# First tile's PSUM copy moved to ScalarE, norm offsets moved to GpSimd, and dummy matmuls behind the first transposes

## The chip, the cores and the metric

The kernel runs on one core of one Trainium2 chip. The metric is the device time of one execution in microseconds (us); lower is better. The profile's span is about 1.8 us shorter than the device time of the same execution. A run is called slow when it is over 1.5% above the fastest run of the same kernel.

A kernel is a list of instructions for five engines: TensorE (PE; its weight loads are PEld), VectorE (DVE), ScalarE (ACT), GpSimd (POOL) and SyncE (SP, which issues the DMAs). The order in which each engine's instructions are issued is not written by hand here. The program is written once from top to bottom, and a list scheduler in the compiler's front end sorts the instructions of each engine by its own cost estimates.

## The reference

The reference is a layernorm, a non-causal linear attention with 32 heads, a residual, a second layernorm and a gated feed-forward part (S = 2048 tokens, D = 1024, F = 3584). Only the beginning matters here.

```python
def _layernorm(x, axis=-1, eps=1e-5):
    m = jnp.mean(x, axis=axis, keepdims=True)
    v = jnp.var(x, axis=axis, keepdims=True)
    return (x - m) / jnp.sqrt(v + eps)

x = A_x
h = x + _A_ref(_layernorm(x, axis=-1), A_wqkv, A_wo)   # qkv = x @ wqkv, phi(k)^T v, ...
h2 = h + _B_ref(_layernorm(h, axis=-1), B_W_gate, B_W_up, B_W_down)
return h2
```

## The kernel before

Sixteen token tiles of 128 rows are normalized and transposed, so that they can be the stationary operand of the k and v products. The first four tiles are transposed by TensorE through PSUM, half by half, the others by DMA. The first four tiles use plain products (`kp`, `vp`). Later ones use Strassen's scheme: seven products of half size, whose operands are sums made on VectorE (`left_sums`, and `sums` in `right_ops`) and whose results are combined from PSUM by ScalarE copies (`m`, `u`, line 154) and VectorE sums (line 211).

```python
# per tile t (lines 266-291)
for k in range(2):
    nc.vector.bn_stats(out=stats[:, k, :], in_=x_sb[:, k * NW:(k + 1) * NW])          # L272
nc.vector.bn_aggr(out=mv[:], in_=stats[:])                                            # L274
nc.scalar.activation(out=lnv, in_=mv[:, 1:2], func=ACT.Ln, bias=LN_EPS, scale=1.0)    # L277
nc.scalar.activation(out=rstd, in_=lnv, func=ACT.Exp, scale=-0.5)                     # L278
if t == atiles[0]:
    ...                                  # tile 0: normalized by VectorE, no offset needed (L283)
nc.vector.scalar_tensor_tensor(out=nmr, in0=mv[:, 0:1], scalar=-1.0, in1=rstd,        # L287, offset
                               op0=ALU.mult, op1=ALU.mult)
nc.scalar.activation(out=xn[:], in_=x_sb[:], func=ACT.Identity, bias=nmr, scale=rstd) # L288
if t not in atiles[:PE_T]:
    nc.sync.dma_start_transpose(out=xT[s][i][:, :, r:r + P], in_=xn[:])               # L290
    return
transpose_in(t, xn)

def transpose_in(t, xn):                                                              # tiles 0 to 3
    for k in range(2):
        pt = pspool.tile([P, KH, P], BF16, tag="D", bufs=1, name="tp")   # one PSUM buffer
        for kc in range(KH):
            nc.tensor.transpose(pt[:, kc, :], xn[:, ...], ident[:])                   # L299
        (nc.scalar.copy if k else nc.vector.tensor_copy)(                             # L300
            out=xT[s][i][:, k * KH:(k + 1) * KH, r:r + P], in_=pt[:])

# Strassen parts
def left_sums(T, S, cols, eng):                                                       # L117-L120
    eng.tensor_tensor(out=s1, in0=a21, in1=a22, op=ALU.add)                           # waits for xT
    ...
def snap(v, nm, bank=A):                                                              # L154
    with tc.high_priority():
        nc.scalar.copy(out=snaps[nm, v], in_=bank[v][:])                              # m, u
# L367: nc.scalar.copy of the plain v products (v_sb)

# start: dummy matmuls while the first loads run
for n in range(SPIN):                                                                 # SPIN = 16
    nc.tensor.matmul(spin[:], lhsT=zero[:, 0:P], rhs=zero[:], start=True, stop=True)  # L400
```

Of the kernel before, what the change touches and what calls it, by code (L numbers as in the profile page):

```python
# [8 lines left out]
ALU = mybir.AluOpType  # L9
# [22 lines left out]
def block_kernel(ctx: ExitStack, tc: tile.TileContext, x, wqkv, wo, wg, wu, wd, out, H: int):  # L32
    nc = tc.nc
    P = 128
# [13 lines left out]
    KH = KC // 2  # L48
# [9 lines left out]
    ident = consts.tile([P, P], BF16, name="ident")  # L58
# [21 lines left out]
    SPIN = 16  # L80
# [147 lines left out]
    with ExitStack() as actx:  # L228
# [11 lines left out]
        def load_x(t):  # L240
            x_sb = bwork.tile([P, D], BF16, tag=("x_res", "oT")[atiles.index(t) % 2], bufs=XB, name="x_sb")
            nc.sync.dma_start(out=x_sb[:], in_=xf[t * P:(t + 1) * P, :])
            x_tiles[t] = x_sb
# [4 lines left out]
        def place(t):  # L248
            i, r = divmod(t * P, HS)
            s, r = divmod(r, SW)  # L250
            return s, i, r
# [3 lines left out]
        atiles = [t for u in units for t in u]  # L255
# [9 lines left out]
        def ln_T(t):  # L265
            if t not in x_tiles:
                load_x(t)
            x_sb = x_tiles.pop(t)
            s, i, r = place(t)
            stats = asmall.tile([P, 2, nc.vector.BN_STATS_DIM], FP32, tag="stats", name="stats")  # L270
            for k in range(2):
                nc.vector.bn_stats(out=stats[:, k, :], in_=x_sb[:, k * NW:(k + 1) * NW])  # L272
            mv = asmall.tile([P, nc.vector.BN_AGGR_DIM], FP32, tag="mv", name="mv")
            nc.vector.bn_aggr(out=mv[:], in_=stats[:])  # L274
            sm = asmall.tile([P, 3], FP32, tag="sma", name="sma")
            lnv, rstd, nmr = (sm[:, k:k + 1] for k in range(3))
            nc.scalar.activation(out=lnv, in_=mv[:, 1:2], func=ACT.Ln, bias=LN_EPS, scale=1.0)  # L277
            nc.scalar.activation(out=rstd, in_=lnv, func=ACT.Exp, scale=-0.5)  # L278
            xn = bwork.tile([P, D], BF16, tag="hn", bufs=HB, name="xn")
            if t == atiles[0]:  # L280
                for k in range(2):
                    ks = slice(k * NW, (k + 1) * NW)
                    nc.vector.tensor_scalar(out=xn[:, ks], in0=x_sb[:, ks], scalar1=mv[:, 0:1], scalar2=rstd,  # L283
                                            op0=ALU.subtract, op1=ALU.mult)
                transpose_in(t, xn)
                return
            nc.vector.scalar_tensor_tensor(out=nmr, in0=mv[:, 0:1], scalar=-1.0, in1=rstd, op0=ALU.mult, op1=ALU.mult)  # L287
            nc.scalar.activation(out=xn[:], in_=x_sb[:], func=ACT.Identity, bias=nmr, scale=rstd)  # L288
            if t not in atiles[:PE_T]:
                nc.sync.dma_start_transpose(out=xT[s][i][:, :, r:r + P], in_=xn[:])  # L290
                return
            transpose_in(t, xn)

        def transpose_in(t, xn):
            s, i, r = place(t)
            for k in range(2):
                pt = pspool.tile([P, KH, P], BF16, tag="D", bufs=1, name="tp")
                for kc in range(KH):
                    nc.tensor.transpose(pt[:, kc, :], xn[:, (k * KH + kc) * P:(k * KH + kc + 1) * P], ident[:])  # L299
                (nc.scalar.copy if k else nc.vector.tensor_copy)(  # L300
                    out=xT[s][i][:, k * KH:(k + 1) * KH, r:r + P], in_=pt[:])

        rk, k_sums = right_ops(wk_sb, tk)
# [91 lines left out]
        with tc.high_priority():  # L395
            zero = asmall.tile([P, NW], BF16, tag="zero", bufs=1, name="zero")
            nc.vector.memset(zero[:], 0.0)
            spin = pspool.tile([P, NW], FP32, tag="A", bufs=2, name="spin")
            for n in range(SPIN):
                nc.tensor.matmul(spin[:], lhsT=zero[:, 0:P], rhs=zero[:], start=True, stop=True)  # L400
            ln_T(atiles[0])
        ln_T(atiles[1])
        todo = atiles[2:8]
        for t in units[0]:
            k_plain(t)
            ln_T(todo.pop(0))
# [30 lines left out]
        for c in range(KC):  # L437
            bnk, i = divmod(c, GPB)
            nc.vector.tensor_tensor(out=kvz[:, c, :], in0=kv_ps[bnk][:, i * NDW:(i + 1) * NDW],
                                    in1=mask[:], op=ALU.mult)  # L440
# [159 lines left out]
    last = rest[-2:]  # L600
# [314 lines left out]
    prv, k = None, 0  # L915
    for r, (wt, f, fi, toks) in enumerate(runs):
        w = [ops() for _, ops in now]
        later = []
        for n, s in enumerate(toks):
# [51 lines left out]
            if k == nwin - 3:  # L971
                for x in range(2):
                    t = wpools[1].tile([P, KC * 2 * GP * P], BF16, tag=("wg", "wu")[x], name="wd")
# [16 lines left out]
    for n in range(2):  # L990
        t = fpool.tile([P, 4 * D], BF16, tag="wraw", bufs=2, name="xd")
# [346 lines left out]
@with_exitstack  # L1338
def kernel(
    ctx: ExitStack,  # L1340
    tc: tile.TileContext,
    A_x: bass.AP,
    A_wqkv: bass.AP,
    A_wo: bass.AP,
    B_x: bass.AP,
    B_W_gate: bass.AP,
    B_W_up: bass.AP,
    B_W_down: bass.AP,
    out: bass.AP,
):  # L1350
    block_kernel(tc, A_x, A_wqkv, A_wo, B_W_gate, B_W_up, B_W_down, out, H=32)
# [30 lines left out]
```

## Time and profile before

| | before |
|---|---|
| device time, median of 3 runs | 740.27 us (739.84 to 740.81) |
| span of the profiled run | 739.5 us |
| TensorE busy | 724.0 us, 98% |
| VectorE / ScalarE / GpSimd busy | 76% / 43% / 1% |

The page gives each engine's busy time, its share of the span and its number of instructions:

```profile
PE 724.0 (98%) x3967; PEld 382.7 (52%) x4020; DVE 563.7 (76%) x992; ACT 321.5 (43%) x580; POOL 5.6 (1%) x44
```

An engine that is busy 98% of the time leaves little to gain, but it is only a mean. The windows view of the same run gives busy time by stretch. Its columns are the stretch, its length, each engine's busy time (and instructions), the granted clock of TensorE, the DMA share and GB/s:

```profile
6.16:9.57 3.41, 1.32 (x9) 0.66 (x8) 2.10 (x5) 0.27 (x2) 0.00 (x0) 1.00 1.08 357
9.57:12.98 3.41, 3.40 (x12) 1.48 (x12) 1.38 (x2) 1.85 (x3) 0.00 (x0) 0.50 1.08 363
41.00:75.00 34.00, 32.34 (x168) 15.27 (x169) 30.16 (x56) 24.32 (x42) 0.85 (x6) 1.00 0.59 147
```

TensorE did 1.32 us of work in the first of these stretches, and in the next one the granted clock was 0.50 (a "slow window" below). The timeline shows why TensorE had so little to do (start, duration, engine, line, operation, and in brackets how long the engine was idle before it and what ended that):

```profile
7.09 0.39 PE L299 MATMUL tp<-ident,xn 128*128 128x128 bf16 x4
7.71 1.29 DVE L272 BATCH_NORM_STATS2 stats<-x_sb 128x6 f32<-128x512 bf16 x2 [1.24 <-DMA x_sb<-in_A_x_dram]
9.16 0.37 DVE L300 COPY xT<-tp 128x512 bf16<-128x512 bf16 x1
9.58 0.58 PE L299 MATMUL tp<-ident,xn 128*128 128x128 bf16 x4 [2.10 <-DVE xT L300]
11.08 0.56 ACT L300 COPY xT<-tp 128x512 bf16<-128x512 bf16 x1
12.94 0.41 PE L299 MATMUL tp<-ident,xn 128*128 128x128 bf16 x4
```

The transposes of tile 0's first half are done at 7.48 us, but the copy that frees their PSUM buffer stands in VectorE's queue behind the statistics of tile 1, which wait for data. TensorE stands for 2.10 us.

Finally the norm offsets, from the view of line 287 (duration minimum/median/maximum in ns), and how long ScalarE waited for them (what, total us, times, longest):

```profile
L287 DVE SCALAR_TENSOR_TENSOR sma<-mv,sma x15: 143/154/159, 9.7 to 63.1; 128x1 f32<-128x1 f32 x15
ACT xn L288 <- DVE sma L287: 4.0, 7, 1.4
```

### The profile page before, as it was taken

The numbers are of one execution on the slowest core, as the hardware profiler recorded it, in microseconds if no ns is written. First come the engines' busy times: TensorE is split into PE (matmuls) and PEld (weight loads), VectorE is DVE, ScalarE is ACT, GpSimd is POOL, SyncE is SP. The second block draws the span as 40 slices with busy tenths as digits, with TensorE's granted clock in tenths as the row PEclk, the third lists the DMA queues.
The fourth block names the chain that finished last, engine by engine and source line by source line (L and its number), as shares of the span: only waits on it lengthen the run. The fifth ranks groups of instructions, "written<-read, shape, count | busy, mean of one in ns | idle before, by whom it ended". The sixth has DMA issues, their size and how long they took to land.

```text
span 739.5 us, 10552 instructions
## 1 busy us (share of the span) xinstructions
PE 724.0 (98%) x3967; PEld 382.7 (52%) x4020; DVE 563.7 (76%) x992; ACT 321.5 (43%) x580; POOL 5.6 (1%) x44
## 2 busy tenths in 40 slices
PE   8999999999999999999999999999999999999997
PEld 3444555444444444444444444444444458888566
DVE  5997644676798767778778777877786479996797
ACT  4877554778887644434344444444445120000000
POOL 0000000000000000000000000000000000000000
PEclk9999999999999999999999999999999999999999
DMA  9666002169987426164638359575583399987822
GB/s 315 153 145 170 1 1 67 48 149 218 237 168 181 124 73 206 43 193 134 198 117 242 110 177 283 171 219 194 170 277 121 129 398 339 331 288 299 295 76 82
DMA packets 146594, 132.02 MB, mean 179 GB/s; under 512 B 50928, under 2 KB 128112, under 8 KB 146544
## 3 DMA queue, kind: packets, MB, share of 16 engines
q1 hardware_dynamic: 135536, 123.30, 55.4%
q10 hardware_dynamic: 11008, 8.06, 3.4%
q8 instruction: 31, 0.51, 0.3%
q14 instruction: 19, 0.16, 0.1%
HBM read 79.95 MB, written 39.85 MB: 162 GB/s over the span
## 4 chain that ended last, share of the span: by engine, by line
PE 78%; DVE 8%; ACT 7%; DMA 5%; issue 1%; SPq 0%; DVEq 0%; POOL 0%; ACTq 0%
PE accA L821 22%; PE accY L821 8%; PE accX L821 8%; PE accA L1153 8%; PE Aq L314 3%; PE accA L982 3%; PE attn L557 3%; PE accX L1153 3%; PE Aq L454 3%; PE accY L1153 2%; DMA hn<-hn 2%; ACT hn L570 2%; PE Eq L314 2%; PE accY L982 2%; PE accX L982 2%
## 5 line engine op out<-in xcount | busy, mean ns | idle before, releaser
L831 ACT ACTIVATE gu<-gu 128x512 bf16<-128x512 bf16 x72 | 45.4, 631 | 131.4 <-DVE gu L830 131.4
L826 ACT COPY snap<-accA 128x1024 f32<-128x1024 f32 x72 | 72.5, 1008 | 36.4 <-PE accA L821 36.3
L821 PEld LDWEIGHTS <-tu 128*128 128x128 f16 x384 | 37.6, 98 | 45.3
L821 PEld LDWEIGHTS <-tg 128*128 128x128 f16 x384 | 37.6, 98 | 45.3
L557 PE MATMUL attn<-wo_mem,oT 128*128 128x512 bf16 x247 | 58.1, 379 | 2.3 <-DVE o_sb L534 1.0
L830 DVE TENSOR_TENSOR gu<-accY,snap 128x1024 bf16<-128x1024 f32 x36 | 43.9, 1220 | 10.0 <-ACT snap L826 10.0
L821 PE MATMUL accA<-hn,tu 128*128 128x512 f16 (+1 forms) x192 | 49.3, 379 | 0.0
L821 PE MATMUL accA<-hn,tg 128*128 128x512 f16 (+1 forms) x192 | 49.3, 379 | 0.0
L830 DVE TENSOR_TENSOR gu<-accX,snap 128x1024 bf16<-128x1024 f32 x36 | 43.9, 1219 | 6.3 <-PE accX L821 3.7
L154 ACT COPY u<-Aq 128x512 f32<-128x512 f32 x54 | 31.1, 580 | 36.2 <-PE Aq L314 19.3
L1153 PEld LDWEIGHTS <-x 128*128 128x128 f16 (+1 forms) x448 | 43.8, 98 | 5.5
L821 PEld LDWEIGHTS <-wg 128*128 128x128 bf16 x288 | 28.2, 98 | 34.0
L821 PEld LDWEIGHTS <-wu 128*128 128x128 bf16 x288 | 28.2, 98 | 34.0
L557 PEld LDWEIGHTS <-oT 128*128 128x128 bf16 x256 | 24.6, 97 | 32.2 <-issue 4.1
L834 DVE TENSOR_TENSOR hq<-gu 128x512 bf16<-128x512 bf16 x48 | 20.3, 423 | 14.3 <-ACT gu L831 14.2
L314 PEld LDWEIGHTS <-xT 128*128 128x128 bf16 (+1 forms) x192 | 18.6, 98 | 23.8 <-issue 2.4
L534 DVE TENSOR_TENSOR o_sb<-nd,rd 128x384 bf16<-128x384 f32 (+1 forms) x48 | 23.2, 509 | 8.6 <-ACT rd L533 6.6
L1153 PEld LDWEIGHTS <-xs 128*128 128x128 f16 x280 | 27.4, 98 | 3.2
L982 PEld LDWEIGHTS <-x 128*128 128x128 bf16 (+1 forms) x168 | 16.5, 98 | 19.6
L560 DVE SCALAR_TENSOR_TENSOR x_res<-attn,x_res 128x512 bf16<-128x512 f32 x32 | 22.0, 686 | 6.1 <-PE attn L557 5.9
L1159 DVE TENSOR_TENSOR snap<-accA,u 128x1024 f32<-128x1024 f32 x16 | 19.5, 1220 | 8.0 <-PE accA L1153 7.9
L821 PE MATMUL accA<-hn,wu 128*128 128x512 bf16 x96 | 24.6, 379 | 0.0
(234 smaller groups left out, 1406.1 us busy)
## 6 DMA issues: line engine op xcount, KB each, us to landing
x<-x_dram SPq DMA_DIRECT2D x17, 896.0 KB, 8.1
x_dram<-hq SPq DMA_DIRECT2D x28, 512.0 KB, 3.0
wg<-in_B_W_gate_dram SPq DMA_DIRECT2D x14, 512.0 KB, 5.1
wu<-in_B_W_up_dram SPq DMA_DIRECT2D x14, 512.0 KB, 7.3
wraw<-in_B_W_down_dram SPq DMA_DIRECT2D x14, 512.0 KB, 4.8
x_dram<-hq SPq DMA_DIRECT2D x28, 256.0 KB, 2.5
t_dram<-wt SPq DMA_DIRECT2D x28, 256.0 KB, 2.2
xd<-x_dram SPq DMA_DIRECT2D x6, 896.0 KB, 7.3
```

Source lines behind the costliest of these rows:

```text
L154: nc.scalar.copy(out=snaps[nm, v], in_=bank[v][:])
L314: nc.tensor.matmul(ps[:], lhsT=left[m - 1][:, kc, r + v * P:r + (v + 1) * P], rhs=right[m - 1][:, kc, :], start=(start and kc == 0), stop= ...
L454: nc.tensor.matmul(ps[:], lhsT=rq[m - 1][:, kc, (c + v) * P:(c + v + 1) * P], rhs=left[m - 1][:, kc, :], start=(start and kc == 0), stop=( ...
L534: nc.vector.tensor_tensor(out=ov[:, c0:c0 + n], in0=ndv[:, :, 0:P].rearrange("p k (h e) -> p k h e", h=HPC), in1=rd[:, 0:n, :].unsqueeze(3 ...
L557: nc.tensor.matmul(ps[:], lhsT=st["oT"][:, c, :], rhs=wo_sb[:, c, j * NW:(j + 1) * NW], start=(c == 0), stop=(c == KC - 1))
L560: nc.vector.scalar_tensor_tensor(out=h_sb[:, j * NW:(j + 1) * NW], in0=ps[:], scalar=1.0, in1=h_sb[:, j * NW:(j + 1) * NW], op0=ALU.mult, ...
L821: nc.tensor.matmul(ps[:, v, :], lhsT=w[v][n - 1][:, kc, :], rhs=left[n - 1][:, kc, :], start=(t is not None and kc == 0), stop=(kc == KH - ...
L826: nc.scalar.copy(out=st[nm][:], in_=halves(st["A"]))
L830: add(out=g[:], in0=halves(st[nm]), in1=st[base][:], op=ALU.add)
L831: nc.scalar.activation(out=g[:, 0, :], in_=g[:, 0, :], func=ACT.Relu)
L982: nc.tensor.matmul(ps[:, t * NW:(t + 1) * NW], lhsT=x_tile(n, s, kh)[:, f, (t0 + t) * P:(t0 + t + 1) * P], rhs=w_tile(n, kh)[:, f, :], sta ...
L1153: nc.tensor.matmul(pv[:, tt, :], lhsT=left(m)[:, f, tt * P:(tt + 1) * P], rhs=right(m)[:, f, :], start=(t is not None and f == 0 and tt % ...
```

## The change

The intent is to close the gap at 7.5 us and to unload VectorE. The copy of the first half of tile 0 goes to the idle ScalarE; eight dummy matmuls behind the first four transposes keep TensorE busy, so that its clock isn't lowered; and the offset `-mean * rstd` of fifteen tiles is computed by GpSimd, which has nothing to do.

```diff
-            nc.vector.scalar_tensor_tensor(out=nmr, in0=mv[:, 0:1], scalar=-1.0, in1=rstd, op0=ALU.mult, op1=ALU.mult)
+            nc.gpsimd.tensor_scalar(out=nmr, in0=mv[:, 0:1], scalar1=rstd, scalar2=-1.0, op0=ALU.mult, op1=ALU.mult)
 ...
             for k in range(2):
                 pt = pspool.tile([P, KH, P], BF16, tag="D", bufs=1, name="tp")
+                if k == 1 and t == atiles[0]:
+                    with tc.issue_after(last.ins):
+                        spin_up(8)
                 for kc in range(KH):
-                    nc.tensor.transpose(pt[:, kc, :], xn[:, ...], ident[:])
-                (nc.scalar.copy if k else nc.vector.tensor_copy)(
+                    last = nc.tensor.transpose(pt[:, kc, :], xn[:, ...], ident[:])
+                (nc.scalar.copy if k or t == atiles[0] else nc.vector.tensor_copy)(
 ...
-            for n in range(SPIN):
-                nc.tensor.matmul(spin[:], lhsT=zero[:, 0:P], rhs=zero[:], start=True, stop=True)
+            def spin_up(n):
+                for _ in range(n):
+                    nc.tensor.matmul(spin[:], lhsT=zero[:, 0:P], rhs=zero[:], start=True, stop=True)
+            spin_up(SPIN)
```

Lines from 299 on have numbers 3 to 7 higher in the changed kernel (L302 are its transposes, L303 their copies, L317 the Strassen products).

More of the change, by code (lines that the diff above doesn't have):

```diff
@@ L297, in transpose_in @@
                 pt = pspool.tile([P, KH, P], BF16, tag="D", bufs=1, name="tp")
+                if k == 1 and t == atiles[0]:
+                    with tc.issue_after(last.ins):
+                        spin_up(8)
                 for kc in range(KH):
-                    nc.tensor.transpose(pt[:, kc, :], xn[:, (k * KH + kc) * P:(k * KH + kc + 1) * P], ident[:])
-                (nc.scalar.copy if k else nc.vector.tensor_copy)(
+                    last = nc.tensor.transpose(pt[:, kc, :], xn[:, (k * KH + kc) * P:(k * KH + kc + 1) * P], ident[:])
+                (nc.scalar.copy if k or t == atiles[0] else nc.vector.tensor_copy)(
                     out=xT[s][i][:, k * KH:(k + 1) * KH, r:r + P], in_=pt[:])
```

## The prediction

> What bounds the kernel now. The page gives PE 724.0 us of 739.5 busy (98%); the front is different. The windows view gives, for 9.57 to 12.98 us, a granted clock of 0.50, with 1.00 on both sides. In the stretch before it (6.16 to 9.57 us) PE was busy 1.32 us only. The Trainium skill, page "TensorE: Matmul & The Clock Gate", Part 1, says that the clock is halved after an idle window of a free-running 3413 ns and restored after a busy one. The trace agrees in the length (3.41 us), and shows that a gap of 2.1 us is enough here.
>
> The cause of the gap (timeline, waits of PE): the transposes of half 0 of the first tile end at 7.48 us, but the VectorE copy of that half runs at 9.16, behind tile 1's statistics (1.29 us, waiting for x until 7.71). The second transposes start at 9.58, in the slow clock; seven kp matmuls take 3.18 us, and tile 1's transposes, whose input was ready at 11.18, start at 12.94.
>
> What the change does.
> 1. The half-0 copy goes to ScalarE, idle from 5.70 to 9.27 us. A ScalarE copy of this form takes 576 ns against 369 to 425 on VectorE, but can run from about 7.5 to 8.1.
> 2. Eight dummy matmuls, 0.216 us each at full clock, occupy PE from about 7.3 to 9.05, so the second transposes start near 9.1, not 8.1; but the window is filled and the clock should stay at 1.00. At half clock 3.41 us do 1.7 us of work: up to 1.7 us gained, and 0.4 to 0.5 from the earlier transposes.
> 3. Offsets on GpSimd: fifteen operations of 154 ns leave VectorE, 97% busy from 13 to 41 us. ScalarE waited 4.0 us for them in seven places; PE was held by one of these chains, 0.5 us at 17.6 (xn of tile 2). I estimate 0.2 to 0.35 us for the GpSimd operation from its 0.18 us one-element copies; VectorE may stretch it, since the skill's "GPSIMD Engine Reference", Specifications, says they share SBUF interfaces.
>
> What is critical. Not all of the 2.1 us survives: the ScalarE copy of half 1 was at 11.08, behind tile 1's normalization (1.24 us). If that order stays, PE waits over 1 us there; the second weight half lands only at 10.7. VectorE, nearly full to 50 us, gains about the 1.4 us that it idled for tile 1's transposes, 0.37 for the copy, and part of 15 x 0.15. So I expect the front to move by 1.5 to 2.2 us, and nearly all of it to reach the end, since later loads are prefetched.
>
> Predicted: 738.4 us (1.9 less, 0.25%), 8 in 10 between 736.8 and 740.0. Faster by over 2%: 0.01; within 2%: 0.98; slower by over 2%: 0.01.
>
> Right if: clock 1.00 from 6.2 us on; half-0 copy on ScalarE near 7.5; second transposes at about 9.1; tile 1's first transposes near 11.5 instead of 12.94; no PE wait for xn of tile 2; the first v matmul (27.29 us before) and the first Strassen matmul (41.10) 1.5 to 2.2 us earlier. Wrong, by step: a slow window still there or displaced; half 1's copy behind tile 1's normalization; GpSimd offsets over 0.5 us, with longer ScalarE waits; a shift at 27 us that is gone by 75 us.
>
> What would make it wrong: the windows' phase differing between runs, so that the kernel before often has no slow window, or the new one still has one; another instruction order; the Strassen part held by transposing DMAs whose times don't move.

## More of the kernel before

Between 26 and 80 us, where the v products and the Strassen products of the first blocks run, TensorE hardly waits. From the waits view (what, total us, times, longest):

```profile
PE Dq L314 <- DVE wo_mem L211: 0.5, 1, 0.5
PE Aq L314 <- ACT u L154: 0.3, 1, 0.3
PE Aq L314 <- ACT m L154: 0.3, 1, 0.3
```

## The result, and the profile after

The changed kernel took 746.5 us (median of 4 runs, 745.27 to 746.81), the kernel before 740.1 us (4 runs). The ratio is 1.0081, with a 95% interval of 1.0066 to 1.0096. It is slower by 0.8%: within 2%, but 6.4 us slower where a gain of 1.9 us was predicted. A ratio here and below is the mean time of one kernel's fast runs over that of the other's of the same rounds, so it is not quite the ratio of the quoted medians.

The windows view of the kernel after, same stretches as before:

```profile
6.16:9.57 3.41, 3.31 (x21) 1.53 (x20) 1.85 (x5) 0.73 (x2) 0.00 (x0) 1.00 1.08 358
9.57:12.98 3.41, 0.95 (x8) 0.69 (x9) 2.06 (x3) 1.98 (x4) 0.27 (x1) 1.00 1.08 363
41.00:75.00 34.00, 30.20 (x153) 14.08 (x155) 25.35 (x45) 23.94 (x42) 4.01 (x12) 0.95 0.66 155
```

The slow window of the front is gone: the clock was 1.00 in both stretches. But TensorE's work fell to 0.95 us in the second one, and between 41 and 75 us it did 2.1 us less than before (30.20 against 32.34) and VectorE 4.8 us less (25.35 against 30.16). The loss is there and just behind it: the first Strassen matmul (L314, L317 after) starts at 40.81 us against 41.10 before, but the first product of the next part (L454, L461 after) at 128.45 against 123.76. So 5.0 us are lost between these two points. The clock of 0.95 comes from one slow window, from 45.30 to 48.71 us. It belongs to the profiled run only; the other three runs of this kernel had a mean clock of 1.000 and the same times, so it isn't the cause of the 6.4 us.

The timeline of the kernel after, for its front:

```profile
6.49 1.89 PE L405 MATMUL spin<-zero 128*128 128x512 bf16 x8
6.69 0.59 ACT L303 COPY xT<-tp 128x512 bf16<-128x512 bf16 x1 [0.94 <-PE tp L302]
8.21 0.39 PE L302 MATMUL tp<-ident,xn 128*128 128x128 bf16 x4
10.27 1.24 ACT L288 ACTIVATE xn<-x_sb,sma 128x1024 bf16<-128x1024 bf16 x1 [0.40 <-POOL sma L287]
11.41 0.56 ACT L303 COPY xT<-tp 128x512 bf16<-128x512 bf16 x1
12.03 0.38 PE L302 MATMUL tp<-ident,xn 128*128 128x128 bf16 x4 [2.56 <-ACT xT L303]
```

The first copy and the dummies do what they should. The copy of the second half, however, still stands behind tile 1's normalization on ScalarE, and TensorE now stands for 2.56 us there. The gap was moved rather than closed: the first v matmul starts at 27.00 us, against 27.29 before. Even that small gain holds only against a run with a slow window: three kernels further below that have the old front, without one, start it at 25.61 to 25.63 us.

The waits of TensorE from 26 to 80 us, kernel after:

```profile
PE Aq L317 <- DMA xT<-xn: 2.4, 1, 2.4
PE Dq L317 <- DVE wo_mem L211: 1.6, 1, 1.6
PE Aq L317 <- ACT m L154: 1.0, 2, 0.7
PE Aq L317 <- ACT u L154: 0.3, 1, 0.3
```

They add up to 5.3 us, where before they were 1.1. The first is named after a DMA, but it ended at 44.20 us, just when ScalarE finished evicting a v product (43.59 to 44.15); that eviction stood behind a normalization that ended at 43.68. So the eviction most likely ended it: in gp_only, below, the same wait (1.9 us) is named after this eviction, and ends 0.05 us after it too. The offsets and ScalarE's wait for them, kernel after:

```profile
L287 POOL TENSOR_SCALAR sma<-mv,sma x15: 257/269/1751, 10.0 to 64.2; 128x1 f32<-128x1 f32 x15
ACT xn L288 <- POOL sma L287: 6.7, 10, 1.5
```

A typical offset takes 269 ns on GpSimd, as estimated, but one took 1751 ns, and ScalarE's wait for offsets rose from 4.0 to 6.7 us.

### The profile page after: what moved, and what is told of

The parts are those of the page before. It is cut to its first block, busy times and chain, and to the rows that moved or that the text cites. A ratio compares the mean times of both kernels' runs of the same rounds, so it can differ in the third digit from the quotient of the medians.

```text
span 744.6 us, 10573 instructions
## 1 busy us (share of the span) xinstructions
PE 724.4 (97%) x3975; PEld 382.8 (51%) x4028; DVE 562.8 (76%) x976; ACT 322.4 (43%) x581; POOL 13.7 (2%) x59
## 4 chain that ended last, share of the span: by engine, by line
PE 75%; DVE 10%; DMA 6%; ACT 5%; issue 2%; SPq 0%; POOL 0%; DVEq 0%; ACTq 0%
PE accA L828 21%; PE accA L1160 8%; PE accX L828 8%; PE accY L828 8%; PE attn L564 4%; PE Aq L317 3%; PE accA L989 3%; PE accX L1160 3%; PE Aq L461 3%; PE accY L1160 2%; PE Eq L317 2%; DMA hn<-hn 2%; ACT hn L577 2%; PE accY L989 2%; PE accX L989 2%
## 5 line engine op out<-in xcount | busy, mean ns | idle before, releaser
L317 PEld LDWEIGHTS <-xT 128*128 128x128 bf16 (+1 forms) x192 | 18.7, 98 | 27.0 <-issue 5.8
L828 PE MATMUL accA<-hs,tg 128*128 128x512 f16 x96 | 24.6, 379 | 0.0
```

Of the source, the lines that this page charges most:

```text
L317: nc.tensor.matmul(ps[:], lhsT=left[m - 1][:, kc, r + v * P:r + (v + 1) * P], rhs=right[m - 1][:, kc, :], start=(start and kc == 0), stop= ...
L828: nc.tensor.matmul(ps[:, v, :], lhsT=w[v][n - 1][:, kc, :], rhs=left[n - 1][:, kc, :], start=(t is not None and kc == 0), stop=(kc == KH - ...
```

## The experiments

The theory after reading the traces: the loss comes from the offsets on GpSimd. There were two ways in which they could cause it, and they had to be told apart. Either GpSimd itself is slow or blocked (theory "latency"), or the scheduler, seeing another engine and another cost, puts the instructions of all engines into another order, and that order is worse on the chip (theory "order"). A rival to both was that the copy or the dummies cost the time. In the expectations, latency is "theory P", order is "theory R", and this rival is "theory O"; A and B are explained where they stand. All kernels below gave correct results.

### One part of the change at a time

gp_only has the first hunk of the diff alone, copy_only the change in the choice of the copy's engine alone, dummies_only `spin_up(8)` alone, copy_dummies the last two.

```diff
# copy_only, whole edit
-                (nc.scalar.copy if k else nc.vector.tensor_copy)(
+                (nc.scalar.copy if k or t == atiles[0] else nc.vector.tensor_copy)(
```

> The kernel before with only the norm offsets moved to GpSimd. Theory P (the GpSimd offsets lengthen the chain statistics - normalization - transposing DMA, because an offset takes 0.27 us there and 1.2 us or more while VectorE runs a two-input operation): 744 to 747 us, as the whole change. Theory O (the loss comes from the front, that is from another instruction order after the copy and the dummy matmuls): within 1 us of 740.

> Only the half-0 copy of tile 0 on ScalarE. Both theories: 739 to 740.5; the second transposes should start about 1 us earlier, and the half clock may be gone or shorter as PE's gap shrinks to about 1.2 us. If it is slower by over 2 us, the copy is part of the cause.

> Only the eight dummy matmuls behind the first transposes. Clock 1.00 through the front. Theory P: 738 to 740. Theory O: 742 or more, since the dummies alone change the order of ScalarE and VectorE up to about 60 us.

> The whole change without its GpSimd part: offsets back on VectorE. Theory P: 737 to 740, that is at least 5 us faster than the whole change. Theory O: 744 or more, like the whole change.

The kernel before took 740.5 us in these rounds (7 runs).

| kernel | median us | ratio to before, 95% interval |
|---|---|---|
| gp_only | 747.11 | 1.0087, 1.0066 to 1.0107 |
| copy_only | 739.98 | 0.9988, 0.9970 to 1.0006 |
| dummies_only | 742.21 | 1.0017, 0.9998 to 1.0036 |
| copy_dummies | 742.54 | 1.0025, 1.0006 to 1.0043 |

The offsets alone cost as much as the whole change. The copy alone is the one part whose mean doesn't lose; the loss of the dummies alone can't be told from none, though their median (742.21) reached the range of theory O. copy_dummies lies between its two ranges: the copy and the dummies together lose about 2 us, not the 6 of the whole change. In the run of copy_only the second transposes started at 8.14 us, without dummies, so the copy is enough to close this gap. There was no slow window in it, but that alone doesn't show that the copy prevents one, as the next traces show.

The seven runs of before also told something about the clock. Their mean clock was 1.000, 1.000, 0.999, 1.000, 1.000 in the runs of 740.08 to 741.08 us, and 0.998 in those of 741.33 and 742.47 us. The profiled run of before that the prediction read was itself one of 0.998, at 741.27 us. A halved clock for 3.41 us lowers the mean by 0.002; so most of these runs had no such window to remove. (A mean doesn't say where in a run a window lay.)

Three kept traces have the old front (but for tile 1's offset, on GpSimd in the first two) and the clock at 1.00 throughout it: gp_only, and gp_before_order and dve_gp_order of the next section. TensorE's gap there was 2.57, 2.31 and 2.28 us, longer than the 2.10 us before which the prediction found "enough". This is the timeline of gp_before_order:

```profile
9.19 0.38 PE L299 MATMUL tp<-ident,xn 128*128 128x128 bf16 x4 [2.31 <-DVE xT L300]
11.48 0.38 PE L299 MATMUL tp<-ident,xn 128*128 128x128 bf16 x4 [0.34 <-ACT xT L300]
```

Tile 1's transposes start at 11.33 to 11.48 us in these three, the first v matmul at 25.61 to 25.63 and the first Strassen matmul at 39.43 to 39.44. In gp_before_order the border between two clock stretches, at 8.37 us, fell inside the gap; TensorE was busy 1.92 us in the one and 2.25 us in the other, against 1.32 us in the one stretch that held nearly all of the gap before. So what the prediction wanted to gain at the front, these runs have without the change. The changed kernel, at 40.81 us in its one trace, is 1.4 us behind them there.

The trace of gp_only shows what a blocked offset looks like (timeline of gp_only; GpSimd, VectorE, ScalarE):

```profile
29.39 1.33 POOL L287 TENSOR_SCALAR sma<-mv,sma 128x1 f32<-128x1 f32 x1 [2.17 <-ACT sma L278]
29.46 1.20 DVE L135 TENSOR_TENSOR pq_mem<-pq_mem 128x2048 f16<-128x2048 bf16 x1
30.75 1.24 ACT L288 ACTIVATE xn<-x_sb,sma 128x1024 bf16<-128x1024 bf16 x1 [1.46 <-POOL sma L287]
```

The one-column offset ended 0.06 us after a VectorE sum with two SBUF inputs had ended. The Trainium skill, page "SBUF — State Buffer", section "SBUF: two separate sides", says that VectorE with two SBUF inputs and a GpSimd operation that reads SBUF need the same pair of ports, that one holds it for its whole instruction, and that the other "fully blocks". The trace agrees: 1.33 us instead of 0.27. One point is left open: the page gives the ports to the one that starts first, and in the profile the offset starts 0.07 us before the sum that blocked it.

### The order and the engine of the offsets, crossed

To separate order from engine, the issue order can be pinned. In the following kernels each engine's instructions are tied together, in a given order, by dependencies that the scheduler obeys and that put no wait into the program:

```python
info = mybir.DependencyInfo(mybir.DependencyClass.NoSync, mybir.DependencyReason.DATA)
for eng, seq in orders.items():          # places in the order of tracing, per engine
    for a, b in zip(seq, seq[1:]):
        tc.add_manual_dep(ins[b], ins[a].name, info, reason="order")
```

gp_before_order has the offsets on GpSimd and the other engines in the order of before. dve_gp_order has the offsets on VectorE and all else in the order that the scheduler chose for gp_only. That the pinning itself costs little is shown by gp_before_order, within 0.4 us of before. (Two further mixtures, ScalarE's order of one kernel with the other engines' order of the other, could not be built: the orders contradict each other.)

> Offsets on GpSimd, but the issue order of all instructions on TensorE, VectorE, ScalarE and the DMA queue is held to that of the kernel before. Theory P (what costs is the GpSimd operation itself: its latency and its collisions with two-input VectorE operations, passed on by ScalarE's fixed order): 744 us or more, as gp_only (747.1). Theory R (what costs is that the scheduler, told of a GpSimd operation, orders the other engines worse): 742 us or less.

> The mirror: offsets on VectorE, but every engine held to the issue order that gp_only had, with each offset in VectorE's order at the place where the scheduler had put it on GpSimd. Theory P: 742 us or less. Theory R: 744 us or more.

| offsets on | order of before | order of gp_only |
|---|---|---|
| VectorE | 740.7 (before, same rounds) | 744.02 (1.0036, 1.0020 to 1.0053) |
| GpSimd | 741.07 (1.0001, 0.9980 to 1.0022) | 747.11 (gp_only, earlier rounds) |

With VectorE making the offsets, the other order costs 3.3 us. In the order of before, moving the offsets to GpSimd costs 0.4 us, which is within the spread. In the other order it costs a further 3.1. But three of gp_only's four runs, and three of these seven of before, had a mean clock of 0.998 or less, and none of dve_gp_order's. Among runs with a clock of at least 0.999 the means are 740.4 and 743.9 us in the first line and 741.2 and 746.1 us (one run) in the second.

The traces show the same without the slow windows. These are the windows of before, gp_before_order, dve_gp_order and gp_only, in this order, each from its first Strassen matmul to the first product of the next part (L454):

```profile
41.10:123.76 82.66, 80.71 (x458) 40.41 (x465) 56.60 (x98) 49.38 (x78) 1.96 (x13) 1.00 0.25 61
39.43:122.75 83.32, 80.97 (x466) 40.36 (x465) 56.72 (x93) 49.35 (x78) 6.17 (x18) 1.00 0.25 61
39.43:126.34 86.91, 80.96 (x465) 40.38 (x464) 57.87 (x100) 49.69 (x77) 1.96 (x13) 1.00 0.24 59
39.44:128.20 88.76, 80.97 (x466) 40.43 (x465) 59.02 (x96) 50.31 (x80) 6.14 (x18) 1.00 0.24 60
```

TensorE's busy time (the third number) is the same within 0.3 us in all four, and its clock is 1.00, so the rest is waiting. The order adds 4.3 us (82.66 to 86.91); GpSimd adds 0.7 us in the old order and 1.9 us in the other. So the order is a cause, and the larger one. GpSimd's latency costs more together with it, but not only then, as after_before_order below shows.

In gp_before_order the blocking occurs too, and it is even longer (timeline; the last line is TensorE):

```profile
40.85 2.33 POOL L287 TENSOR_SCALAR sma<-mv,sma 128x1 f32<-128x1 f32 x1 [3.67 <-ACT sma L278]
41.91 1.22 DVE L135 TENSOR_TENSOR wv_sb<-wv_sb 128x2048 f16<-128x2048 bf16 x1
43.22 1.24 ACT L288 ACTIVATE xn<-x_sb,sma 128x1024 bf16<-128x1024 bf16 x1 [1.50 <-POOL sma L287]
44.98 1.02 PE L314 MATMUL Aq<-pq_mem,xS 128*128 128x512 f16 x4 [1.76 <-ACT m L154]
```

The offset met the sum of line 134 (40.78 to 41.99) and stayed blocked through the next one, until 43.18. TensorE lost 1.76 us there, yet had little else to wait for (0.4 us more between 26 and 80 us).

What is wrong with the other order? This is dve_gp_order (timeline), where GpSimd plays no part:

```profile
47.19 0.69 DVE L117 TENSOR_TENSOR xS<-xT 128x1024 f16<-128x1024 bf16 x1 [1.85 <-DMA xT<-xn]
50.80 0.20 DVE L274 BATCH_NORM_AGGREGATE mv<-stats 128x2 f32<-128x12 f32 x1
51.69 1.24 ACT L288 ACTIVATE xn<-x_sb,sma 128x1024 bf16<-128x1024 bf16 x1 [0.23 <-DVE sma L287]
52.84 1.05 ACT L154 COPY u<-Aq 128x512 f32<-128x512 f32 x2
53.45 1.89 PE L314 MATMUL Aq<-pq_mem,xT 128*128 128x512 f16 x8 [1.88 <-ACT u L154]
```

VectorE stands at a left sum that waits for a transposing DMA, with the statistics of another tile ready behind it. So these are aggregated at 50.80 us (47.51 before). ScalarE stands at the normalization that needs them, with two ready evictions of `u` behind it. And TensorE stands 1.88 us for those. The Trainium skill, page "PSUM — Partial Sum Buffer", section "Engine vs sequencer instructions", calls the queues of these engines "strict FIFO"; the trace shows that order of events.

### Making the latency larger

gp_twice pins the order of gp_only and makes each offset with two chained GpSimd operations.

```diff
-nc.gpsimd.tensor_scalar(out=nmr, in0=mv[:, 0:1], scalar1=rstd, scalar2=-1.0, op0=ALU.mult, op1=ALU.mult)
+nc.gpsimd.tensor_scalar(out=half[:], in0=mv[:, 0:1], scalar1=rstd, scalar2=None, op0=ALU.mult)
+nc.gpsimd.tensor_scalar(out=nmr, in0=half[:], scalar1=-1.0, scalar2=None, op0=ALU.mult)
```

> gp_only's issue order held, each offset made by two chained GpSimd operations in place of one (the cost in question doubled, nothing else moved). Theory P: 2 to 5 us slower than gp_only, about 749 to 752. Theory R: as gp_only within 1 us.

It took 753.31 us (1.0171, 1.0142 to 1.0201), 6.2 us more than gp_only; between 26 and 80 us ScalarE waited 10.9 us for offsets (6.2 in gp_only). But its four runs had mean clocks of 0.986 to 0.997. In the profiled run, at 0.993, three slow windows (45.22 to 52.05 and 69.11 to 72.53 us) followed two long gaps of TensorE (4.48 and 3.27 us). In the stretch from the first Strassen matmul to L454, which took 5.3 us more than in gp_only (94.04 against 88.76), TensorE was busy 4.3 us longer, at the low clock, and waited only 1.0 us more; the first v matmul came 1.1 us later. So the latency does reach TensorE in that order, but in the profiled run most of the difference was a lowered clock, behind gaps that were long enough for it. What the second operation costs by itself can't be read from it.

### Removing the collisions

gp_fence keeps the order of gp_only and lets the two VectorE sums that ran into an offset wait until that offset is done.

```diff
+for sums, offset in ((292, 256), (450, 413)):   # L135 of the k weights and of the v weights
+    tc.add_manual_dep(ins[sums], ins[offset].name, mybir.DependencyInfo(
+        mybir.DependencyClass.Sync, mybir.DependencyReason.DATA), reason="no collision")
```

> The issue order of the kernel with only the offsets moved (747.1 us), with two added waits: the two long VectorE operations with two inputs that overlapped a stretched GpSimd offset in that run (starting at 29.46 and 42.98 us) now wait until that offset is done. Theory A, the two engines block each other and the stretched offsets (1.33 and 1.70 us instead of 0.27) hold the normalizations behind them: both fall to about 0.3 us, TensorE's waits in 26 to 60 us shrink by 1 to 2 us in sum, time 744.5 to 746.3. Rival B, the collisions cost nothing beyond what the order already costs: time 746.5 to 748, TensorE's waits as before.

It took 746.04 us, ratio 1.0056 (1.0028 to 1.0083). The first of the two offsets is now short (timeline of gp_fence):

```profile
29.51 0.27 POOL L287 TENSOR_SCALAR sma<-mv,sma 128x1 f32<-128x1 f32 x1 [2.18 <-ACT sma L278]
37.32 2.49 POOL L287 TENSOR_SCALAR sma<-mv,sma 128x1 f32<-128x1 f32 x2 [2.67 <-ACT sma L278]
```

The second fell from 1.70 to 0.36 us, but a pair at 37.32 us, 1.01 us long in gp_only, was now 2.49 us long. The interval overlaps that of gp_only, and the chip of these rounds was a noisier one (before: 741.5 us median, up to 744.11). The time lies in the range that the theory of collisions had expected, and TensorE's waits between 26 and 80 us fell from 7.8 us in gp_only to 6.5, but the profiled run had a slow window too. So this run does not settle what the collisions cost.

### Repairing the order, place by place

gp_evict_first keeps gp_only and its order, except that on ScalarE five PSUM evictions (one of v, four of m and u) are moved ahead of three normalizations that they stood behind.

```diff
 ScalarE's order in gp_only, by line number
-... L288(xn) L367(v) L278 L288(xn) L367(v) L154(m) ... L277 L278 L288(xn) L154(u) L154(u) ...
+... L367(v) L288(xn) L278 L367(v) L154(m) L288(xn) ... L154(u) L154(u) L277 L278 L288(xn) ...
```

> Offsets on GpSimd and the same issue order as the 747.1 us kernel on TensorE, VectorE and SyncE; on ScalarE five PSUM evictions (one v copy, four copies of Strassen products m and u) are moved ahead of three normalizations of x that stood before them. Theory A, ScalarE's in-order queue made TensorE wait for evictions stuck behind normalizations that themselves waited for statistics and offsets: TensorE's waits for v_sb, m and u in 26 to 60 us (6.97 us in sum in the 747.1 us run) fall by 3 us or more, time 741 to 744.5. Rival B, the lost time comes from the offsets' latency, or from VectorE's order, and only shows up at the evictions: the waits come back under other names, time 745.5 to 748.

It took 748.35 us (1.0082, 1.0055 to 1.0108). The expectation of 741 to 744.5 missed. TensorE's waits came back under other names: 3.5 us for m, and 3.5 us for VectorE's product sums (L211), which now were the ones behind the left sum that waited 2.15 us for its DMA. An eviction early in ScalarE's queue helps nothing if the consumer's next step is late in VectorE's queue.

So the next five kernels changed VectorE's order at that place. dve_stats_first is dve_gp_order with the other half of the statistics, their aggregation and one product sum moved ahead of the left sum; gp_stats_first does the same in gp_only; gp_stats_evict_first has this and gp_evict_first's move. dve_chain_first moves, besides, the offset that follows from these statistics to the place right behind the first left sum. dve_chain_evict_first adds, on ScalarE, two v evictions and one m eviction ahead of the normalizations.

```diff
 VectorE's order in dve_gp_order, by line number
-L272 L211 L117(waits) L272 L118 L211 L119 L120 L274 L272 L287(offset) ...
+L272 L211 L272 L274 L211 L117 L118 L119 L120 L272 L287(offset) ...      # dve_stats_first
+L272 L211 L272 L274 L211 L117 L287(offset) L118 L119 L120 L272 ...      # dve_chain_first
```

> Offsets back on VectorE, issue order of the offsets-only kernel (that pair ran 0.36% slower than before), with one change in VectorE's order: the second half of one tile's statistics, its aggregation and one product sum of the first Strassen block are issued ahead of the left sums of the second row group, which waited 1.85 us for a transposing DMA in that order. Theory A, VectorE's in-order queue stood at that wait with ready work behind it (aggregation at about 51 us instead of 47.5, so the next normalization and the u copies behind it on ScalarE came late): aggregation near 47.5 to 48.5, TensorE's wait of 1.9 us for u gone, sum of its waits in 26 to 80 us from 6.0 to 3.5 us or less, ratio to before 1.0025 or less. Rival B, the loss lies in ScalarE's or TensorE's order: ratio 1.003 to 1.005.

> The same change of VectorE's order in the kernel with the offsets on GpSimd (1.0087 before). Theory A: the aggregation moves from 52.3 to about 48 us, TensorE's waits in 26 to 80 us fall from 7.8 us by 2 to 4, ratio 1.003 to 1.006; what remains is the stretched GpSimd offsets at 38 and 42.5 us. Rival B: ratio 1.007 or more.

> Both repairs of the order: VectorE's as above and ScalarE's evictions ahead of three normalizations (which alone gave 1.0082, its waits reappearing at VectorE's product sums). Theory A, each repair failed or gave little alone because the other queue was blocked too: ratio 1.0005 to 1.004, TensorE's waits in 26 to 80 us under 4 us. Rival B: ratio 1.006 or more.

> As dve_stats_first (1.0058), and the offset that follows from the moved statistics is issued right behind the first left sum, as in the order of before, instead of behind all four and another statistics. In dve_stats_first that offset was made at 51.08 us though its rstd was ready at 47.3; ScalarE stood 3.9 us at the normalization for it, with two ready u evictions behind it, and TensorE waited 1.63 us for those. Theory A (head of a queue blocked, handed from VectorE to ScalarE to TensorE): normalization near 48.5 us, u evictions not behind it any more, the wait of 1.63 us gone, ratio 1.002 to 1.0045. Rival B (something else holds this part): ratio 1.005 or more.

> The same, and on ScalarE one v eviction and one m eviction (with the v eviction before it) ahead of the two normalizations that they stood behind, as in the order of before; TensorE waited 0.99 us for v and 1.39 us for m there. Theory A: both waits under 0.6 us, ratio 1.0 to 1.0025, so that three local places of the order account for nearly all of the order's cost. Rival B: ratio 1.004 or more, the cost lies elsewhere in the order.

| kernel | median us | before, same rounds | ratio, 95% interval |
|---|---|---|---|
| dve_stats_first | 744.19 | 740.17 | 1.0058, 1.0044 to 1.0072 |
| gp_stats_first | 748.42 | 740.17 | 1.0105, 1.0089 to 1.0121 |
| gp_stats_evict_first | 746.35 | 740.17 | 1.0087, 1.0073 to 1.0100 |
| dve_chain_first | 743.13 | 740.76 | 1.0039, 1.0018 to 1.0061 |
| dve_chain_evict_first | 742.51 | 740.76 | 1.0023, 1.0002 to 1.0043 |

The first three missed: moving the statistics gained nothing. In the two with the offsets on GpSimd, stretched offsets near 38 and 43 us (2.1 to 2.5 us long) stayed as well. The trace of dve_stats_first says why (timeline):

```profile
45.79 0.21 DVE L274 BATCH_NORM_AGGREGATE mv<-stats 128x2 f32<-128x12 f32 x1
51.08 0.14 DVE L287 SCALAR_TENSOR_TENSOR sma<-mv,sma 128x1 f32<-128x1 f32 x1
51.26 1.24 ACT L288 ACTIVATE xn<-x_sb,sma 128x1024 bf16<-128x1024 bf16 x1 [3.93 <-DVE sma L287]
52.40 1.05 ACT L154 COPY u<-Aq 128x512 f32<-128x512 f32 x2
53.02 1.24 PE L314 MATMUL Aq<-pq_mem,xT 128*128 128x512 f16 x5 [1.63 <-ACT u L154]
```

The aggregation is 5 us earlier, but the 0.14 us offset still stood behind all four left sums. ScalarE waited for it with the same two evictions behind, and TensorE waited with it. A chain of small operations is as late as its worst-placed link. In dve_chain_first that offset was moved too, and the two events follow as expected (timeline):

```profile
49.54 1.24 ACT L288 ACTIVATE xn<-x_sb,sma 128x1024 bf16<-128x1024 bf16 x1 [1.41 <-DVE sma L287]
50.69 0.56 ACT L154 COPY u<-Aq 128x512 f32<-128x512 f32 x1
```

TensorE's wait for u is gone from its list of waits, and the ratio fell from 1.0058 to 1.0039. With the evictions moved as well it fell to 1.0023: TensorE's wait for v (1.0 us) is gone, that for m at 44 us fell from 1.50 to 0.59 us. But dve_stats_first was itself no better than dve_gp_order (1.0036), whose order is being repaired. From 1.0036 to 1.0023 is 1 us, and the intervals overlap. The stretch from the first Strassen matmul to L454, with the clock at 1.00 in all these traces, shortened from 86.91 us (dve_gp_order) to 86.21, 85.93 and 85.30, against 82.66 before. So the three places account for about 1.6 of 4.3 us, by one trace each. About 2.6 us remain; TensorE's largest waits there are 1.18 us for m at 59.69 us and 1.24 us for a product sum at 74.90 us, other places of the same order, which no experiment touched. The last expectation, that three places account for nearly all of the order's cost, isn't borne out, although the ratio fell in its range.

### The whole change without its new order

after_before_order is the whole change, with all four engines in the order of before; the new copy stands right behind tile 0's rstd on ScalarE, the dummies right behind the first transposes. copy_dummies_before_order is the same with the offsets on VectorE.

> The whole change (copy, offsets and dummies), but TensorE, VectorE, ScalarE and SyncE issue in the order of the kernel before; the half-0 copy stands right behind the first rstd of tile 0 on ScalarE, the dummies right behind the first four transposes. Theory A, the loss of 6 us comes from the rearranged order and the change itself is worth about nothing: 739.3 to 741.5. Rival B, the copy, the dummies or the offsets cost the time themselves: 744 or more.

> The half-0 copy on ScalarE and the eight dummies, offsets on VectorE, issue order of before on all engines (the copy right behind tile 0's rstd, the dummies right behind the first four transposes). It is the whole change in that order without GpSimd: the whole change in that order was 743.3 us, 3.1 us slower than before where only runs with a clock of at least 0.999 are compared. Theory A, what remained there was the GpSimd offset stretched to 1.86 us at 41.2, and copy and dummies cost nothing in this order: 739.3 to 741.2 us, first Strassen matmul near 39.3, no wait over 0.6 us for m near 45. Rival B, the dummies cost time themselves (with the scheduler's own order, copy and dummies ran 742.5): 742 us or more.  In either case the runs with a clock of at least 0.999 are compared.

after_before_order took 743.32 us against 741.5 (1.0019, 0.9995 to 1.0043), in the rounds on the noisier chip. That is about 3 us better than the changed kernel (measured in other rounds), but outside the expected 739.3 to 741.5. Among runs with a mean clock of at least 0.999, it took 743.5 us in the mean (3 runs) against 740.4 (6 runs). copy_dummies_before_order took 740.93 us against 740.38 (1.0007, 0.9994 to 1.0019): with the order of before, the copy and the dummies cost nothing that can be seen, where the scheduler's own order for them gave 1.0025 (the intervals overlap). What remained in after_before_order is then most likely GpSimd's, although the offsets alone in this order (gp_before_order) cost 0.4 us, with an interval up to 0.2%. From the first Strassen matmul to L454 after_before_order took 84.62 us and copy_dummies_before_order 83.07, so GpSimd cost about 1.6 us there without the new order, against 0.7 in gp_before_order. Its trace has an offset of 1.86 us at 41.20 us, and TensorE waited 1.28 us for m at 44.85. The same place without GpSimd, from the waits of copy_dummies_before_order:

```profile
PE Aq L317 <- ACT m L154: 0.2, 1, 0.2
```

### Looking for a version faster than both

copy_act_nmr is copy_only with the offset made by ScalarE, from a negated mean that VectorE writes. copies_first is copy_only in the order of before, with both copies of tile 0 on ScalarE ahead of everything for tile 1.

```diff
 # copy_act_nmr
-nc.vector.scalar_tensor_tensor(out=nmr, in0=mv[:, 0:1], scalar=-1.0, in1=rstd, op0=ALU.mult, op1=ALU.mult)
+nc.scalar.activation(out=nmr, in_=negm, func=ACT.Identity, scale=rstd)   # negm = -mean, by VectorE
 # copies_first, ScalarE's order by line number
-L277(t0) L278(t0) L277(t1) L278(t1) L288(t1) L300(t0, half 1) ...
+L277(t0) L278(t0) L300(t0, half 0) L300(t0, half 1) L277(t1) L278(t1) L288(t1) ...
```

> A try at a better version: half-0 copy on ScalarE as in copy_only (739.98); the offset is made by ScalarE itself from a negated mean that VectorE writes right behind the mean, so that no answer has to come back from another engine after rstd. Theory P: 738 to 740.5, since the 4.0 us that ScalarE waited for the offsets shrink, against about 15 x 0.2 us of new ScalarE work. Theory R gives no number; the order changes again, so up to 742.

> The half-0 copy alone (offsets on VectorE, no dummies), order of the kernel before on all engines, but with both transposed copies of tile 0 on ScalarE ahead of everything that ScalarE does for tile 1. If the front's gap costs time one for one: second transposes near 8.1 us, tile 1's transposes 1.5 to 2.5 us earlier than 12.94, and the time 738.0 to 739.6, faster than both kernels. Rival: the front's gain is taken back by later waits (weights, VectorE) before the first Strassen product, and the time stays at 739.7 to 741.

copy_act_nmr took 741.32 us against 740.7 (1.0005, 0.9987 to 1.0023). copies_first took 742.02 us against 741.5 (1.0005, 0.9982 to 1.0029). Neither beats the kernel before, and copies_first lies above both ranges that were expected for it (copy_act_nmr above that of theory P). In copies_first the front works as intended: tile 1's transposes start at 11.19 us instead of 12.94, the first v matmul at 25.6 instead of 27.29, the first Strassen matmul at 39.44 instead of 41.10. But this is measured against a profiled run with a slow window. Its profiled span was 738.4 us at a clock of 0.999; five runs of the kernel before with a clock of 1.000, in the same rounds, had spans of 737.9 to 739.7. No profile of the kernel before without the slow window was at hand, but gp_before_order has its front in its order: there the first v matmul starts at 25.61 us and the first Strassen matmul at 39.43. So by these traces the front's 1.7 us was the slow window's; the earlier copies by themselves brought nothing that is left at the first Strassen matmul. (In copy_only, in the scheduler's order, it starts at 39.03 us, 0.4 us earlier.) The lowest is copy_only, at 0.9988, which cannot be told from 1.

## Why the prediction was wrong

- "The half-0 copy goes to ScalarE ... can run from about 7.5 to 8.1": right in kind. It ran right behind the transposes, from 6.69 to 7.28 us, and took 0.59 us.
- "the window is filled and the clock should stay at 1.00 ... up to 1.7 us gained": the clock did stay at 1.00 at the front. The size failed, because the profiled run of before was one with a slow window, and most of the other runs have none. That "a gap of 2.1 us is enough here" held for that run, not for the kernel: three traces with gaps of 2.28 to 2.57 us at the same place kept a clock of 1.00. The prediction named the risk ("the windows' phase differing between runs") but kept the gain in its sum. The Trainium skill, page "TensorE: Matmul & The Clock Gate", Part 1, says that the window is free-running and the effect "run-variable"; the runs of before agree, with mean clocks from 0.994 to 1.000. A run at 0.998 took 741.33 us, one at 1.000 took 740.08.
- "Not all of the 2.1 us survives: the ScalarE copy of half 1 was at 11.08, behind tile 1's normalization ... If that order stays, PE waits over 1 us there": it stayed, and TensorE waited 2.56 us. So tile 1's transposes came at 12.03 us, not at 11.5, and the first v matmul was 0.29 us earlier instead of 1.5 to 2.2. This term was mis-sized by more than 1.2 us. Against the old front without a slow window (25.61 to 25.63 us), the changed kernel's front was later by 1.4 us, by one trace.
- "VectorE ... gains ... part of 15 x 0.15", the third step, failed in its sign. Moving the offsets alone cost 6.6 us (gp_only), half of it or more by the order that came with them. VectorE's 154 ns operations became GpSimd operations of 269 ns as estimated, but up to 1751 ns when a sum with two inputs held VectorE; the page names the shared interface, and the prediction had said that VectorE "may stretch it", without a size.
- "I expect ... nearly all of it to reach the end": the largest failure. The prediction took the order of issue as given. It listed "another instruction order" among the risks, at no weight. With the offsets still on VectorE, the order that the scheduler made for gp_only cost 3.3 us (dve_gp_order); the order that it made for the copy and the dummies took 1.0025, against 1.0007 in the order of before. These orders put normalizations and left sums, which wait for others, ahead of evictions and statistics that were ready.
- "the Strassen part held by transposing DMAs whose times don't move" came close to what was seen: a left sum waiting for such a DMA was one of the places. But what held TensorE was what stood behind it in VectorE's queue.

What the runs showed is then: the order that came with the offsets, 3.3 us; the offsets on GpSimd in that order, 2 to 3 us more (gp_only less dve_gp_order, from different rounds: 3.1 by the medians, 2.2 by the runs with a clock of at least 0.999, 1.9 in the stretch to L454); the copy and the dummies, within 0.1% once the order is held. That these parts add up to the whole change's 6 us isn't claimed: the changed kernel has an order of its own. For it, after_before_order shows that about 3 us of 6.4 go with the order; the rest is argued from the other kernels. Still open are how GpSimd's share divides between plain latency and blocking, and 2.6 us of the order's cost.

## What to carry to other kernels

Where a scheduler sorts the instructions, a change to one small operation is a change to the order of all; before crediting or blaming the operation, pin the order of the old kernel and run the operation alone, and run the new order with the old operation. When an in-order queue blocks TensorE, move the whole chain of ready work (statistics, aggregation, offset, eviction) ahead of the waiting instruction; moving one link gained nothing here, and repairing three places won back less than half. And before counting on a window of low clock, look at the granted clock of several runs, because a profile is one of them. The same holds for an experiment: gp_twice looked like 6.2 us of latency, and in its profiled run 4.3 of them were a lowered clock.

## What the Trainium skill lacked or had wrong

- "SBUF — State Buffer", section "SBUF: two separate sides", says that the loser blocks for the winner's whole instruction. Here the loser could also be blocked through two instructions of the winner in a row: the offset at 40.85 us in gp_before_order lasted 2.33 us, through a VectorE sum that ended at 41.99 and the next one that ended at 43.13.
- "GPSIMD Engine Reference", Specifications, names the shared interface, but none of its figures there says what a one-column operation takes: 0.27 us free, here, against 0.15 us for VectorE's own, and up to 2.33 us when blocked by sums of 1.2 us.
- "TensorE: Matmul & The Clock Gate", Part 1, says that the low clock follows an idle window. In the profiled run of the kernel before, a stretch in which TensorE was still busy for 1.32 of 3.41 us was followed by a window at 0.50. Cut into such stretches of 3.41 us where the clock record puts them, and without the start and the end of the runs, all traces together show nine from which the clock fell; TensorE was busy 0.00 to 1.59 us in these, and 1.47 us or more in all others at full clock. Five of the eleven runs of one series of the kernel before had a mean clock of 0.998 or less.
- No page read here says that the order of issue must be held fixed to measure one instruction's cost; here it was worth 3.3 us of 740 (dve_gp_order).
